# A fused attention and MLP kernel: products written in place and gathered from there, and a plan over two batches and the first channel MLP

## The chip, the cores and the metric

The kernel runs on one core of a Trainium2 chip. The metric is the device time of one execution in microseconds (us), the median of the runs shown; lower is better. The core has TensorE (PE; PEld is its weight load), VectorE (DVE), ScalarE (ACT), GpSimd (POOL) and SyncE (SP), which here issues nearly all DMA transfers.

## The reference

Batch 4, 8 heads, sequence 768, head dimension 48, model width 384. Three parts follow each other.

- Attention as a recurrence with a complex decay per channel: the decay's magnitude is clipped at 0.999, the state takes `k v` at each step, and `q` reads the state's real part.
- A mixer: `u = x + (U V)` applied along the sequence (rank 32, the "token mix"), then a channel MLP, `u + relu(u w_ch1) w_ch2` with 1536 hidden columns.
- A second mixer: `theta = x w_theta`, `x cos(theta)` and `x sin(theta)` go through two 768x768 matrices along the sequence, and a channel layer with relu is added.

```python
new_re = ar * S_re - ai * S_im
new_im = ar * S_im + ai * S_re
S_re, S_im = (new_re + kv, new_im)
y[:, :, t] = np.einsum('bhd,bhde->bhe', q[:, :, t], S_re)
...
h = xt @ U @ V
u = x + h.transpose(0, 2, 1)
ch = np.maximum(u @ w_ch1, 0.0) @ w_ch2
```

## The kernel before

The recurrence is worked in chunks of 128 positions, six to a batch, with attention matmuls inside a chunk and a carried 48x48 state per head between chunks. The decay's powers come from a scan of the magnitude and a scan of the angle.

**Preparing a pair of chunks** (`ew`, L276, on 128x768 tiles). `load` (L254) brings four rows `re`, `im`, `q`, `kk`, in three transfers for each of the two chunks, the last with q and k together. ACT squares, takes reciprocal roots, arctangent and sine; DVE multiplies and scans (L315 for the magnitude, L346, three times, for the angle). Four more rows A, B, C, D are used for the squares first and for the sine and cosine at the end. POOL clears a column of `dec` (L298), copies the scan's last column (L324, choice of POOL or ACT) and writes a sentinel column into the product buffer (L370). For each chunk, `prod` (L374) multiplies q and k by the sine and by the cosine, into a buffer `SRC` of its own: there is one such buffer, and a second for the odd chunks of batch 0. `gather` (L380) moves each half to the tile `QK` by five transfers on SP (L387 to L391), so ten for a chunk.

**A chunk on PE** (`pe_steps`, L405): scores (L431), which ACT copies (L437) and POOL masks (`affine_select`, L441); transposes of k (L447, copied by ACT at L399); the state (L470); the output (L496, and L499 for the carried state), copied into `x` by ACT (L399); and the first half of the token mix (L511). After six chunks, `g_steps` (L524) closes the token mix: one evacuation by ACT (L530) and one by DVE (L533), six matmuls (L541) and six additions on DVE (L546).

**Weights.** `unpack` (L553) turns 64-bit weights into a high and a low fp32r part: one load, five integer steps (L573 to L580; the first may go to ACT, at L574), a cast on ACT (L587), and the low part, `lo = value - hi`, which may go to POOL or DVE (L588, recorded at L272). Nine such jobs make `w1`, twelve make `w2`, one `U` and one `V`. Their staging is memory of `x` of batch 1. The second mixer's weights are unpacked the same way after the attention of batch 3 (lane `w3`).

**The channel MLP** of a batch (`mains`, L759) has 18 units: `f_unit` (18 matmuls of 128x256 at L659; ACT makes the high part with relu at L664, DVE the low part at L665) and `c_unit` (12 matmuls of 128x384 at L680), one unit behind. Before every six units `prologue` transposes x (L641) and splits it (L645, L646).

**What sets the order.** `startup` (L719) collects the steps of batch 0's attention (`PLANNED = 1`), the token mix and the weights. `schedule` (L80) gives each step an engine and a place: it takes ready steps in the order of a rank (the table `LEAD`) and puts each into the first free gap on its engine's line, even ahead of steps placed before. `fixed` (L689) emits them in that order and ties each DVE, ACT and POOL instruction to the one before it on its engine (`HELD`, L688); PE and SP aren't tied. Everything else is emitted in lanes of falling priority, `evac a0 a1 a2 a3 w3 moe p2 mix fill`, and the framework's list scheduler may put it between the planned steps: attention of batch 1 in lane `a1`, the MLPs in `moe`, and so on, where the attention of a batch stands above the MLP of the batch ahead of it.

## Time and profile before

| What | Value |
|---|---|
| median of 3 runs | 890.32 us (889.41 to 893.34) |
| the profiled execution | 890.87 us, of which the span is 889.0 us |
| PE busy | 772.3 us, 87% of the span |
| DVE busy | 534.5 us, 60% |
| ACT busy | 437.2 us, 49% |
| POOL busy | 214.7 us, 24% |
| DMA | 79.69 MB, mean 90 GB/s |

The busy shares are means over stages that differ. The span has three: the start-up, in which batch 0's attention and the weights are made ready; the stretch in which the MLPs and the attention of batches 1 to 3 share PE; and the second mixer from 655 us on. The granted clock is a share of TensorE's full 2.4 GHz; 0.5 stands for 1.2 GHz, values between are means.

### The profile page before, as it was taken

Reading aid. Unit: us, or ns where it says so; the run is one execution under the profiler, and the core shown is the slowest. Engines: PE = TensorE matmul, PEld = TensorE weight load, DVE = VectorE, ACT = ScalarE, POOL = GpSimd, SP = SyncE. Lnnn points to the kernel's source line nnn. Section 1 sums busy time; section 2 is a strip of 40 time slices with the busy share of each in tenths; the row PEclk is TensorE's granted clock in tenths of the full one; section 3 lists DMA queues with packets and bytes.
Section 4 is the critical chain, followed back from the end, with each engine's and each line's share of the span. In section 5 each row is a group of like instructions: output and inputs, shape, how many; then the busy total and the mean of one; then the engine's idle time right before and its main releaser. Section 6 shows DMA issues by size and latency. Waiting matters only on the chain.

```text
span 889.0 us, 13548 instructions
## 1 busy us (share of the span) xinstructions
PE 772.3 (87%) x5242; PEld 745.9 (84%) x5242; DVE 534.5 (60%) x763; ACT 437.2 (49%) x703; POOL 214.7 (24%) x218
## 2 busy tenths in 40 slices
PE   0167565689999989999999899999999999999996
PEld 0166454689889889898998899999999999999996
DVE  7989979994857748867177785332234434354321
ACT  5766836484946956965233442221145435343300
POOL 2032443232202112313012232000044424224200
PEclk9996765899999999999999999999999999999999
DMA  9345646434443434452216741000050000000001
GB/s 250 104 120 156 191 128 171 114 84 116 107 116 81 126 100 113 110 125 52 83 54 209 237 159 37 1 1 1 1 204 11 28 27 1 27 27 28 28 28 31
DMA packets 104889, 79.69 MB, mean 90 GB/s; under 512 B 32144, under 2 KB 96656, under 8 KB 104816
## 3 DMA queue, kind: packets, MB, share of 16 engines
q1 hardware_dynamic: 104416, 78.55, 31.7%
q8 instruction: 43, 0.70, 0.3%
q14 instruction: 30, 0.25, 0.1%
q10 hardware_dynamic: 400, 0.20, 0.1%
HBM read 50.33 MB, written 9.44 MB: 67 GB/s over the span
## 4 chain that ended last, share of the span: by engine, by line
PE 51%; DVE 17%; ACT 14%; DMA 7%; issue 4%; SPq 4%; POOL 2%; DVEq 0%; POOLq 0%; ACTq 0%
PE c L680 9%; PE h L659 9%; PE h L906 8%; PE c L906 8%; ACT et L293 4%; PE m L855 4%; PE m L922 4%; PE m L496 2%; SPq L387 2%; ACT L293 2%; DVE SRC L272 2%; PE m L499 2%; DVE et L296 2%; DMA tok1l<-tl 1%; DMA ei<-in_pk_dram 1%
## 5 line engine op out<-in xcount | busy, mean ns | idle before, releaser
L659 PE MATMUL h<-uh,w1h 128*128 128x256 f32 x432 | 123.7, 286 | 5.1 <-DVE ul L646 4.1
L659 PE MATMUL h<-uh,w1l 128*128 128x256 f32 x432 | 122.8, 284 | 0.0
L659 PE MATMUL h<-ul,w1h 128*128 128x256 f32 x432 | 122.6, 284 | 0.2 <-DVE ul L646 0.2
L665 DVE SCALAR_TENSOR_TENSOR rl<-h,rh 128x512 fp32r<-128x512 f32 x72 | 49.6, 688 | 102.7 <-ACT rh L664 102.4
L680 PE MATMUL c<-w2h,rl 128*128 128x384 f32 x288 | 99.9, 347 | 0.8 <-DVE rl L665 0.7
L680 PE MATMUL c<-w2l,rh 128*128 128x384 f32 x288 | 99.1, 344 | 0.0
L680 PE MATMUL c<-w2h,rh 128*128 128x384 f32 x288 | 95.7, 345 | 0.8 <-ACT rh L664 0.8
L431 PE MATMUL m<-QK 96*128 96x128 f32 x384 | 56.8, 298 | 44.3 <-DMA QK<-SRC 40.5
L664 ACT ACTIVATE rh<-h 128x512 fp32r<-128x512 f32 x72 | 42.9, 598 | 104.0 <-PE h L659 103.9
L431 PEld LDWEIGHTS m<-QK 96*128 96x128 f32 x384 | 52.1, 210 | 48.8 <-issue 44.2
L659 PEld LDWEIGHTS h<-uh,w1h 128*128 128x128 f32 x432 | 81.4, 188 | 6.7 <-DVE ul L646 5.0
L659 PEld LDWEIGHTS h<-ul,w1h 128*128 128x128 f32 x432 | 81.4, 188 | 0.7 <-DVE ul L646 0.4
L659 PEld LDWEIGHTS h<-uh,w1l 128*128 128x128 f32 x432 | 81.4, 188 | 0.3
L496 PE MATMUL m<-vt,pt 128*128 128x96 f32 x384 | 64.9, 298 | 2.5 <-POOL pt L441 2.4
L441 POOL TENSOR_SCALAR_AFFINE_SELECT pt<-pt 128x512 f32<-128x512 f32 x48 | 46.6, 978 | 75.9 <-ACT pt L437 75.5
L470 PE MATMUL m<-vt,kn 128*96 128x96 f32 x320 | 38.7, 272 | 25.5 <-ACT kn L399 24.6
L272 DVE TENSOR_TENSOR SRC<-ei,et 128x768 f32<-128x768 f32 x40 | 41.3, 1071 | 31.7 <-POOL SRC L370 30.7
L470 PEld LDWEIGHTS m<-vt,kn 128*96 128x96 f32 x320 | 34.3, 182 | 30.9 <-ACT kn L399 28.7
L496 PEld LDWEIGHTS m<-vt,pt 128*128 128x128 f32 x384 | 56.8, 213 | 3.8 <-POOL pt L441 3.8
L680 PEld LDWEIGHTS c<-w2h,rl 128*128 128x128 f32 x288 | 54.7, 190 | 2.2 <-DVE rl L665 2.0
L680 PEld LDWEIGHTS c<-w2l,rh 128*128 128x128 f32 x288 | 54.7, 190 | 0.3
L680 PEld LDWEIGHTS c<-w2h,rh 128*128 128x128 f32 x288 | 53.1, 189 | 1.4 <-ACT rh L664 1.0
(210 smaller groups left out, 1910.9 us busy)
## 6 DMA issues: line engine op xcount, KB each, us to landing
QK<-SRC SPq DMA_DIRECT2D x84, 144.6 KB, 3.4
ei<-in_pk_dram SPq DMA_DIRECT2D x44, 192.0 KB, 2.9
ei<-in_pk_dram SPq DMA_DIRECT2D x22, 384.0 KB, 3.8
x<-in_moe_w_ch_dram SPq DMA_DIRECT2D x9, 512.0 KB, 4.5
vt<-in_v_dram SPq DMA_DIRECT2D x24, 192.0 KB, 3.1
x<-in_moe_w_ch_dram SPq DMA_DIRECT2D x12, 384.0 KB, 3.8
st<-in_moe_w_tok_i_dram SPq DMA_DIRECT2D x6, 768.0 KB, 5.3
st<-in_moe_w_tok_r_dram SPq DMA_DIRECT2D x6, 768.0 KB, 4.2
```

Of the source, the lines that this page charges most:

```text
L272: ENG[e].tensor_tensor(**kw)
L293: do("A", size, r, w, lambda e: A_.activation(out=out, in_=in_, func=func, **kw), tab)
L431: PE.matmul(ps[:, hh * T:(hh + 1) * T], lhsT=st["QK"][:, h, T:2 * T], rhs=st["QK"][:, h, 0:T], start=True, stop=True)
L441: G_.affine_select(out=pt, in_=pt, pattern=[[0, 4], [1, T]], compare_op=ALU.is_ge, fill=0.0, base=0, channel_multiplier=-1)
L470: PE.matmul(ps[0:96, r * 96:(r + 1) * 96], lhsT=st["kn"][:, h, :], rhs=vw(h), start=(z == 0), stop=(z == 1))
L496: PE.matmul(o, lhsT=st[f"pt{h // 4}"][:, h % 4, :], rhs=vw(h), start=(z == 0), stop=(z == 1 and c == 0))
L659: PE.matmul(ps[:, f, :], lhsT=a[:, k, fs], rhs=u[:, k, :], start=(k == 0 and i == 0), stop=(k == NJ - 1 and i == 2))
L664: A_.activation(out=rh, in_=ps, func=AF.Relu)
L665: V_.scalar_tensor_tensor(out=rl, in0=ps, scalar=0.0, in1=r32(rh), op0=ALU.max, op1=ALU.subtract)
L680: PE.matmul(ps[t][:, 0:C], lhsT=r[:, f, t * T:(t + 1) * T], rhs=w[:, k, :], start=(k == 0 and i == 0), stop=(k == KF - 1 and i == 2))
L855: PE.matmul(ps[:, 0:C], lhsT=a[:, k, :], rhs=ww[:, k, :], start=(k == 0 and i == 0), stop=(k == NJ - 1 and i == 2))
L906: PE.matmul(ps[k][:, 0:C], lhsT=z[:, 2 * part + o, k * 128:(k + 1) * 128], rhs=w[:, s, ts], start=(s == 0 and part == 0 and j == 0), stop= ...
```

## The change

- **Rows and products.** The pair's store becomes twelve padded rows of 6x129 elements; q and k, and C and D, lie beside each other, so that the products of a chunk are written in place: with the sine into C and D, with the cosine into q and k. `gather` reads from there; `SRC` is gone. There is a second row for `im`, used by pairs in turn, and rows `n` and `sq` that the angle and the square use. The column that POOL cleared is cleared once at the start. The sentinel and the copy of the scan's last column are always on ACT. q and k, and the halves of the value tile, are loaded by transfers of their own.
- **Unpacking.** The first step is always on ACT, the low part always on DVE. Staging moves to the memory of batch 2's `x`.
- **The plan.** `PLANNED = 2`, and the first batch's MLP (`mlp_steps`) is part of it, each piece a step with its own keys (`w1` by column group, `w2` by row block, the PSUM banks `ph` and `pc`). `schedule` goes forward in time: among the ready steps that could start within 400 ns of the earliest, it takes the one of lowest rank, and nothing is put ahead of a step already placed. Ranks are a step's distance from the end along its dependencies plus `LEAD`, which has new values. `HELD` stays the same.

```diff
-PLANNED = 1
+PLANNED = 2
...
-def schedule(steps, rank, bias, hop=HOP, banks=4, pf=1.3, warm=1e5):
+COST = {"V": (150, 1.042), "A": (180, 0.833), "G": (150, 2.1), "P": (0, 1.0), "D": (0, 1)}
+BANKS = {"ps": 4, "ph": 2, "pc": 2}
+def schedule(steps, rank, bias, hop=HOP, window=400):
...
+            cand.append((best, n))
+            low = min(low, best[1])
+        (_, st, en, e), n = min((c for c in cand if c[0][1] <= low + window), key=lambda c: (rank[c[1]], c[1]))
...
+def ranks(steps, names, lead, hop=HOP):
...
+        up[n] += a + b * size + hop[e]
+        for m in pre[n]:
+            up[m] = max(up[m], up[n])
...
+        out.append((top - up[n]) / 1000 + r0 + dr * k / names.count(nm))
...
-    stg = [xf[:, NC * C + i * 1536:NC * C + (i + 1) * 1536] for i in range(3)]
-    src2 = xf[:, B * NC * C - NJ * 2 * (2 * T + 1):]
+    stg = [xf[:, PLANNED * NC * C + i * 1536:PLANNED * NC * C + (i + 1) * 1536] for i in range(3)]
...
+    ROWS = ("re", "im", "q", "kk", "A", "B", "C", "D", "dec", "n", "sq", "im1")
+    er = ac.tile([128, len(ROWS), NR], F32, name="er")
...
-    EU = 'AV'
+    EU = 'A'
...
-        for lo, hi, names in ((0, 1, ("re",)), (1, 2, ("im",)), (2, 4, ("q", "kk"))):
+        zi = (1, 11)[pr % 2]
+        for z, name in enumerate(("re", ROWS[zi], "q", "kk")):
...
+            for z in range(2):
+                nc.sync.dma_start(out=vt[:, :, 2 * z, :], in_=v[b, z::2, c * T:(c + 1) * T, :].rearrange("r s e -> s r e"))
...
-        do("G", 3, [], K("dec"), lambda e: G_.memset(dec[:, :, :, 0:1], 0.0))
...
-        do("GA", 6, K("dec"), [("pc", pr)], pcs)
+        do("A", 6, K("A"), [("pc", pr)], lambda e: A_.copy(out=pcf[:, pr], in_=rows[4][:, :, T]))
...
+        for a, key in (("qk", "kk"), ("cd", "D")):
+            do("A", 6, K("C"), K(key), lambda e, a=a: A_.mul(
+                out=st[a][:, :, 1, T], in_=st["cd"][:, :, 0, T - 1], mul=P2_0 ** -0.5))
...
-            do("GA", 6, K("C"), [sk + "0", sk + "1"], src)
...
+            for cs, to, a, keys in ((1, "cd", n2, ("C", "D")), (0, "qk", Bt, ("q", "kk"))):
+                kc = K(*[(x, i) for x in keys])
+                tt2(st[to][:, i::2, :, 0:T], st["qk"][:, i::2, :, 0:T],
+                    a[:, i::2].rearrange("p j (o t) -> p j o t", o=1).to_broadcast([128, NJ, 2, T]), ALU.mult,
+                    K("q", "kk", ("q", i), ("kk", i), "nB"[cs == 0]), K(*(keys if i == 0 else ())) + kc)
+                do("D", 3250, kc + K(*keys), [f"qk{g % 2}{cs}"], lambda e, g=g, cs=cs: gather(e, g, cs))
...
-        do("GV", n, lambda e: tt(e, out=lo, in0=tv, in1=r32(hi), op=ALU.subtract), w)
+        do("V", n, lambda e: tt(e, out=lo, in0=tv, in1=r32(hi), op=ALU.subtract), w)
...
+    def mlp_steps(b):
...
+            do("P", 18 * 119, [("u", n % 2)] + [("w1", p // 2, k) for k in range(NJ)], [m], mm)
+            do("A", 512, [m], [kr], hi)
+            do("V", 512, [m, kr], [kr, m], lo)
...
+                do("P", 6 * 174, [kr, ("w2", 2 * p), ("w2", 2 * p + 1)], [m], lambda e, t=t: mm(e, t))
...
+        ops = mlp_steps(0)
+        steps.extend(ops)
+        names.extend("m0" if o[1] == "P" else "mv" for o in ops)
+        rank = ranks(steps, names, LEAD)
         done = schedule(steps, rank, BIAS)
...
-        mains(b)
+        if b:
+            mains(b)
```

## Rows read from the trace of the kernel before

**Rows 1.** The page, part 4: the chain that ended last, by engine.
```profile
PE 51%; DVE 17%; ACT 14%; DMA 7%; issue 4%; SPq 4%; POOL 2%; DVEq 0%; POOLq 0%; ACTq 0%
```

**Rows 2.** Stretches: length; PE, PEld, DVE, ACT, POOL busy; granted clock; DMA; GB/s.
```profile
0.00:169.00 169.00, 81.72 (x472) 72.73 (x472) 147.73 (x206) 108.53 (x155) 54.83 (x63) 0.78 0.59 156
40.50:90.00 49.50, 37.08 (x223) 34.20 (x224) 44.90 (x57) 31.94 (x50) 15.61 (x16) 0.82 0.51 138
90.00:138.00 48.00, 28.70 (x182) 25.90 (x180) 40.39 (x61) 26.85 (x40) 21.94 (x15) 0.68 0.60 163
138.00:169.00 31.00, 15.95 (x70) 12.60 (x70) 29.31 (x47) 22.57 (x33) 10.27 (x10) 0.57 0.47 134
169.00:655.00 486.00, 464.21 (x3450) 448.11 (x3451) 296.04 (x399) 241.72 (x372) 87.74 (x86) 1.00 0.33 90
655.00:889.00 234.00, 226.33 (x1322) 225.02 (x1320) 90.69 (x159) 86.99 (x178) 72.10 (x70) 0.99 0.13 41
```

**Rows 3.** Timeline of PE, 0 to 230 us; in brackets wait and releaser.
```profile
118.21 1.59 PE L470 MATMUL m<-vt,kn 128*96 128x96 f32 x8 [14.52 <-ACT kn L399]
...
169.42 0.39 PE L659 MATMUL h<-uh,w1h 128*128 128x256 f32 x1 [3.06 <-DVE ul L646]
```

**Rows 4.** The chain of waits between 85 and 175 us: start, length, what.
```profile
88.03 1.82 DVE x L272 x2
...
160.91 1.40 DVE x L546 x3
```

**Rows 5.** Timeline of SP's queue, 80 to 200 us: start, length, issue.
```profile
100.62 0.65 SPq L387 DMA_DIRECT2D QK<-x  x1
```

**Rows 6.** Timeline of POOL, 85 to 200 us.
```profile
103.15 10.35 POOL L324 COPY pcf<-dec 128x6 f32<-128x6 f32 x1 [4.83 <-DVE dec L315]
```

**Rows 7.** The page, its part 6: DMA issues, KB each, us to landing.
```profile
QK<-SRC SPq DMA_DIRECT2D x84, 144.6 KB, 3.4
ei<-in_pk_dram SPq DMA_DIRECT2D x44, 192.0 KB, 2.9
ei<-in_pk_dram SPq DMA_DIRECT2D x22, 384.0 KB, 3.8
```

**Rows 8.** Groups of DVE, 0 to 190 us: count, busy us, mean ns, idle.
```profile
L578 DVE SCALAR_TENSOR_TENSOR x<-x 128x384 uint32<-128x384 uint32 x12 | 10.1, 840 | 0.2
...
L272 DVE TENSOR_TENSOR ei<-ei,et 128x768 f32<-128x768 f32 x8 | 7.3, 952 | 0.0
L315 DVE TENSOR_TENSOR_SCAN dec<-dec,d 128x774 f32<-128x774 f32 x4 | 7.1, 1764 | 0.1
L272 DVE TENSOR_TENSOR ei<-ei,et 128x1536 f32<-128x1536 f32 x4 | 7.0, 1752 | 0.0
...
L573 DVE TENSOR_SCALAR x<-x 128x384 uint32<-128x384 uint32 x10 | 3.9, 394 | 0.0
...
L346 DVE TENSOR_TENSOR_SCAN et<-ones,ei 128x256 f32<-128x256 f32 x6 | 3.7, 669 | 0.3 <-ACT ei L343 0.3
...
L546 DVE TENSOR_TENSOR x<-x,m 128x384 f32<-128x384 f32 x6 | 3.0, 547 | 0.0
...
L272 DVE TENSOR_TENSOR w1l<-x,w1h 128x512 fp32r<-128x512 f32 x3 | 2.0, 675 | 1.8 <-ACT w1h L587 1.8
```

**Rows 9.** DVE's busy time on staging and x, 169 to 190 us.
```profile
169.00:190.00 21.00, 11.66 (x19) 1.00 0.42 114
```

**Rows 10.** Groups of POOL over the span, columns as in 8.
```profile
L272 POOL TENSOR_TENSOR w2l<-x,w2h 128x384 fp32r<-128x384 f32 x12 | 14.6, 1216 | 31.7 <-ACT w2h L587 31.6
...
L272 POOL TENSOR_TENSOR w1l<-x,w1h 128x512 fp32r<-128x512 f32 x6 | 9.3, 1544 | 13.8 <-ACT w1h L587 13.8
```

**Rows 11.** The chain of waits between 545 and 565 us, in the MLPs alone.
```profile
557.10 2.11 PE c L680 x12
559.21 2.13 PE h L659 x18
```

**Rows 12.** Who waited for whom over the span: us, times, longest.
```profile
DVE SRC L272 <- POOL SRC L370: 30.7, 13, 6.3
```

More of the change, by code (lines that the diff above doesn't have):

```diff
@@ L89, in schedule @@
             succ[m].append(n)
-    uses = {}
+    uses, psn = {}, []
     for _, _, _, r, w, _ in steps:
-        for k in {*r, *w}:
-            if k[0] == "ps":
-                uses[k] = uses.get(k, 0) + 1
-    psn = [sorted(k for k in {*s[3], *s[4]} if k[0] == "ps") for s in steps]
-    bank, free = {}, [0.0] * banks
-    line = {e: ([], [], []) for e in "VAGPD"}
-    end = [0.0] * len(steps)
-    heap = [(rank[n], n) for n in range(len(steps)) if not left[n]]
-    heapq.heapify(heap)
-    out, wait = [], []
@@ L149, in schedule @@
         out.append((st, n, e, en))
+        ready.remove(n)
         for k in psn[n]:
@@ L517, in pe_steps @@
         gk = [gps["k"]] if b else []
[L519 to L520 removed]
+        mix.append(step(lambda e: copy(e, xs[b][:, c, :], st["y"][:, 0:C]), "A", 384, [m], [m, ("x", b, c)]))
         mix.append(step(gx, "P", 660, [("x", b, c), "u4"], [kg] + gk))
@@ L759, in mains @@
     def mains(b):
-        units = [(n, p) for n in range(NB) for p in range(KF // 2)]
-        prologue(b, 0)
-        for i, (n, p) in enumerate(units):
-            f_unit(b, n, p)
-            if i:
-                c_unit(b, *units[i - 1])
-            if p == 3 and n + 1 < NB:
-                prologue(b, n + 1)
-        c_unit(b, *units[-1])
+        for f, e, *_ in mlp_steps(b):
+            with lane("moe" if e == "P" else "evac"):
+                f(e)
     with lane("a0"):
```

428 lines of the change are left out of this document (219 added, 209 removed), and 23 rows, old and new, of the table LEAD.

## The prediction

> **What bounds the kernel now.** I read the chain that ended last first, to see which engine holds the end. It is TensorE for 51% of the span, VectorE (DVE) for 17%, ScalarE (ACT) for 14% [rows 1]. The stretches then show where each rules [rows 2]. From 169 us to 655 us PE is busy 464.2 of 486 us, and from 655 us to the end 226.3 of 234: 690.5 us of work and 29.5 us of idle time, at a granted clock of 0.99 to 1.00. There only less PE work or less idle time helps, and the change takes no PE work out. Before 169 us it is otherwise: PE is busy 81.7 us at a clock of 0.78, while DVE is busy 147.7 of 169 us. So the first 169 us belong to DVE and to the order of the work, and the question is when the first channel MLP, the start of the full stretch, can begin.
>
> The timelines of single engines say why it begins only at 169.4 us [rows 3]. The last products of batch 0 are done at 89.85 us [rows 4], 79.6 us earlier. What should follow is one gather, one chunk of attention and the token mix. Instead, the gather of the last chunk is issued at 100.62 us [rows 5]; a 128x6 copy of batch 1 holds the POOL queue for 10.35 us [rows 6], with a mask of batch 0 and the sentinel fill behind it; a matmul of batch 0 then waits 14.52 us, because the copy that feeds it stands in ACT's fixed order behind a weight cast, which waits for DVE, which waits for that fill [rows 3]; and the last three additions of the token mix come at 160.91 us [rows 4], behind steps of batch 1. Batch 1 is not in the plan of before: its instructions are put between the planned ones, on queues whose order the plan has fixed.
>
> **The change part by part.**
>
> *Batch 1 and the first MLP in the plan.* By the trace's durations the tail after 89.85 us needs: ten gather issues at about 0.63 us, 6.3 [rows 5]; landing 3.4 [rows 7]; about 5 us of PE (a whole chunk is at most 15.95 x 0.57 = 9.1 us at full clock, the PE time of 138 to 169 us [rows 2]); and eight evacuations of about 0.6 us [rows 8], 4.8; with hand-overs some 12 us after the landing. That is 111.5 us; I take 115 for the MLP's start, as some of this will not run freely. Ends: 105 if batch 0's products also come earlier, 145 if the weights go ahead of them.
>
> *What DVE must do first.* The MLP's first six units need all first- and second-layer weights. DVE has spent 147.7 us by 169, of which batch 1 took some 32. A pair of chunks costs 13 steps of 0.952, one of 1.752, a scan of 1.764 and three of 0.669: 17.9 us [rows 8]; pair 3 whole and pair 4 without its four products (3.8) make 32. Another 11.7 us of weight steps lie behind 169 [rows 9]. So 147.7 - 32 + 11.7 = 127 us. The change adds the low-half subtractions that POOL had: 6 x 0.675 + 12 x 0.547 = 10.6 us. It takes away the first unpack step, 14 times about 0.394: 5.5 us [rows 8]; ACT gets those, busy 108.5 of 169 us [rows 2], and has room. And what POOL's subtractions cost DVE goes: the 12 shifts of 384 columns took 0.840 us where another two-input step of that size took 0.547 [rows 8], 3.5 us in this one group. Ends for all groups: 0, and the 23.9 us that POOL spent there [rows 10]; I take 7, twice the one group, since other groups beside it show less. 127 + 10.6 - 5.5 - 7 = 125 us. At the share that DVE reached while the plan ran alone, 44.9 of 49.5 [rows 2], with 5 us for the MLP's own evacuations, that is 130 / 0.907 = 143 us; for what the two batches get out of order I add 5: 148.
>
> The shift row also bears on a rule. The Trainium skill ("SBUF — State Buffer", section "Who interferes with whom") says that a DVE instruction with two SBUF inputs contends with a GpSimd instruction that reads SBUF, and that the later one is blocked for the whole instruction. By it most of POOL's 23.9 us would be DVE's loss, the weights would be ready some 17 / 0.907 = 19 us sooner, and the sum would lose the 7.6 us of idle time below: 850 us; 0.840 against 0.547 agrees with the rule in direction, not in that size.
>
> *PE between 115 and 148.* It can do six units at 2.13 + 2.11 us [rows 11], 25.4 of 33 us: 7.6 idle. At a clock of 0.82, which 75% busy had [rows 2], they still fit.
>
> *Rows of their own, products in place.* The single product buffer goes; DVE waited 30.7 us for its fill in 13 places [rows 12], most of them after 169 us, where the MLP covers them (PE 95.5% busy): nothing there. Next pair's squares no longer write over this pair's angles. New waits: the loads of the next q and k stand behind this pair's gathers on SP. That is 3.2 us of issue, 3.4 to land, 2.9 to load [rows 7], about 10, while DVE needs eight steps and a scan, 9.4 us [rows 8], to reach the product that reads them: 0, with 2 us in each of five planned pairs as the other end, 10. Behind those loads SP holds value loads and weight loads, which are an iteration early. ACT gets three small copies a pair that POOL had; the POOL queue keeps only the masks, so no mask stands behind a scan any more.
>
> *More and smaller transfers.* q and k split 384 KB into two of 192 KB, and each value load becomes two: 24 more in the plan's 6 pairs. SP pays at most 0.65 us an issue [rows 5], 16 us spread over some 250, hidden by its idle time; 2 x 2.9 in place of 3.8 us [rows 7], 2 us a pair, is the other end, 12 us if each pair waits. The Trainium skill ("DMA: Bandwidth & Descriptors", section "Rules for kernel authors") tells to coalesce transfers, which speaks against this edit; were its fixed cost of about 2 us paid by each pair, the sum would be 12 us higher, the same as that end.
>
> *After 148 us.* PE has 12 units (51 us) and six chunks (8 us each: 100 together), DVE three pairs (54) and some 39 additions and low halves of 0.55 us or more (22): 76 against 100, PE bound again. For an order that is now fixed on three engines I add the idle share of the whole middle, 4.5%, once more: 5 us. The low halves of the last weights move from POOL to DVE too, under the MLPs of 455 to 600 us: nothing.
>
> **Sum.** From the MLP's start: 690.5 us, one chunk more that was already done at 169 (8), idle 29.5 + 7.6 + 5 = 42: 741. 115 + 741 = 856 us of span, against 889.0; with the 1.87 us that lie around the span in the profiled run (890.87), 858. The median of the three runs is 0.55 lower than that run, which I leave aside.
>
> **The rivals.**
> 1. *The weights go first.* The start moves to 145 us only, as DVE's bill must be paid anyway; the 7.6 us fall away: 145 + 733 = 878, 880 us. For it: DVE is the fuller engine before 169. Against: the first unit needs three of nine first-layer pieces.
> 2. *Slower: the fixed order starves PE.* In the planned stretch after 115 us lie 18 units and six chunks, 76 + 49 = 125 us of PE work, on three queues that cannot overtake. The forecast gives them about 145 us, 86% (with 7 us of the middle's idle time). At the 60% of 90 to 138 us (28.7 of 48) they need 209: 64 more, 922 us. At the 75% of 40.5 to 90, 167: 22 more, 880. Slower by 0.5% begins at about 69%. For it: the 14.52 us wait was such a queue [rows 3]. Against: that wait came from steps outside the plan.
> 3. *Better.* Start at 105 us, no idle time for weights, half of the middle's idle time saved: 105 + 698.5 + 29.5 - 10 = 823 of span at best, 825; with half of these gains, about 838.
> 4. *It does not do what it says.* PE's order is not among the held ones; if its matmuls of the MLP are queued behind waiting ones of batch 1, the start stays near 165 us: 890.
>
> **How the numbers follow.** Forecast 0.58, with 838 to 872 from the two 10 to 12 us ends and 105 to 125 us of start; rival 1 0.18 (872 to 886); rival 3 0.09; rival 2 0.10; rival 4 0.05. A measurement of this kernel tells about 0.5% from no change (its three runs differ by 0.4%). Faster takes the forecast, rivals 1 and 3 nearly whole, 0.84; same 0.06; slower 0.10. The range leaves out part of rivals 2 to 4: 834 to 886.
>
> **What would show it.** The first MLP matmul between 105 and 125 us; no POOL subtraction of weights, shifts near 0.56 us; DVE's weight steps done by about 150 us; PE busy over 85% from 115 to 260 us at a clock of 1.0; the work after the first MLP's end unchanged in length. A start after 140 us, or a share below 70% there, would make the prediction wrong.

## The result, and the profile after

The changed kernel takes 877.24 us (median of 4 runs, 876.67 to 877.70) where the kernel before takes 890.81 (889.41 to 893.34, 4 runs): a ratio of 0.9844, 95% interval 0.982 to 0.9868. That is 13.6 us faster. The forecast was 858 us and 33 us of gain; the direction holds, the size does not.

The chain that ended last, by engine, as in [rows 1]: TensorE (PE) holds more of it than before.

```profile
PE 59%; DVE 17%; DMA 8%; ACT 7%; SPq 4%; issue 4%; POOL 1%; DVEq 0%; ACTq 0%
```

Stretches of the changed kernel, columns as in [rows 2]:

```profile
0.00:131.00 131.00, 63.05 (x416) 57.19 (x416) 108.96 (x152) 95.33 (x149) 17.97 (x36) 0.86 0.60 160
131.00:181.00 50.00, 48.41 (x364) 46.88 (x364) 40.78 (x78) 24.44 (x46) 3.24 (x4) 0.96 0.45 127
181.00:238.00 57.00, 56.20 (x402) 54.92 (x403) 46.16 (x59) 39.74 (x64) 2.13 (x2) 1.00 0.27 72
238.00:290.00 52.00, 39.65 (x227) 34.88 (x226) 33.72 (x45) 27.05 (x45) 6.89 (x7) 0.73 0.41 100
290.00:400.00 110.00, 105.23 (x818) 99.91 (x818) 85.46 (x113) 74.59 (x127) 16.69 (x13) 0.99 0.44 112
400.00:500.00 100.00, 98.84 (x766) 95.53 (x765) 47.86 (x77) 37.68 (x64) 7.57 (x10) 1.00 0.33 90
500.00:640.00 140.00, 135.64 (x929) 134.22 (x928) 72.67 (x109) 46.75 (x75) 2.57 (x3) 0.98 0.25 87
640.00:875.00 235.00, 227.87 (x1332) 226.48 (x1330) 90.62 (x159) 86.54 (x177) 71.84 (x70) 1.00 0.13 41
```

From 131 to 238 us PE is full (104.6 of 107 us). Then comes what the kernel before does not have, a hole: from 238 to 290 us PE is busy 39.65 of 52 us, at a granted clock of 0.73, and DVE idles too, 33.72 busy of 52. From 290 us on PE is nearly full again (105.23 of 110).

The PE timeline, as in [rows 3]: the first MLP matmul starts at 131.40 us in place of 169.42.

```profile
106.55 2.13 PE L451 MATMUL m<-QK 96*128 96x128 f32 x16
...
114.31 1.17 PE L516 MATMUL m<-vt,pt 128*128 128x96 f32 x4 [5.62 <-POOL pt L461]
...
131.40 0.58 PE L696 MATMUL h<-uh,w1h 128*128 128x256 f32 x1 [1.68 <-DVE ul L677]
```

To see where the head start goes I count work. The number of matmuls of each kind in a stretch, times what one takes at full clock (0.119 and 0.1755 us for the two products of the MLP, 2.13/18 and 2.11/12 [rows 11]; 0.086 to 0.325 us for attention's kinds), gives the full-clock work that PE has done by a given time, out of 503 us in all before the second mixer:

| by (us) | 131 | 181 | 238 | 290 | 400 | 500 | 640 |
|---|---|---|---|---|---|---|---|
| before | 41.3 | 64.6 | 117.9 | 164.5 | 264.8 | 360.6 | 485.1 |
| after | 47.2 | 92.9 | 148.7 | 175.3 | 277.4 | 375.3 | 500.1 |
| ahead | 5.9 | 28.3 | 30.8 | 10.8 | 12.6 | 14.7 | 15.0 |

The head start reaches 30.8 us of work, close to the forecast gain, and 20 us of it are given back between 238 and 290 us. The rest stays to the end. So there are two questions: what made the head start, and why it was lost in that hole.

Who does what around the hole stands in DVE's timeline: the last low half of the weights and the magnitude scan of pair 4 behind it, the last addition of the first MLP, the first token-mix addition of batch 1.

```profile
181.37 0.55 DVE L309 TENSOR_TENSOR w2l<-x,w2h 128x384 fp32r<-128x384 f32 x1
181.84 1.76 DVE L356 TENSOR_TENSOR_SCAN er<-er,d 128x774 f32<-128x774 f32 x1
...
238.29 0.54 DVE L726 TENSOR_TENSOR x<-x,c 128x384 f32<-128x384 f32 x1
...
282.60 1.02 DVE L566 TENSOR_TENSOR x<-x,m 128x384 f32<-128x384 f32 x2
```

The first MLP is done at 238 us, 112 us earlier than before (350). The second may only start behind batch 1's token mix, which begins at 283 us, 21 us later than before (261.4). In the plan pair 4 of batch 1 stands behind the weights: its scan, now at 181.84 us, came at 152.08 in the kernel before:

```profile
152.08 1.76 DVE L315 TENSOR_TENSOR_SCAN dec<-dec,d 128x774 f32<-128x774 f32 x1
...
397.36 1.75 DVE L315 TENSOR_TENSOR_SCAN dec<-dec,d 128x774 f32<-128x774 f32 x1
```

The second of these lines is the scan of the last pair of batch 3. After the change it comes at 391.18 us:

```profile
391.18 1.76 DVE L356 TENSOR_TENSOR_SCAN er<-er,d 128x774 f32<-128x774 f32 x1
```

The MLP began 38 us earlier, but the last scan of attention came only 6 us earlier, and the token mixes of batches 1, 2 and 3 began 21, 29 and 18 us later (table below).

### The profile page after: what moved, and what is told of

Same layout as the page of the kernel before. It is cut to its first block, busy times and chain, and to the rows that moved or that the text cites. A ratio compares the mean times of both kernels' runs of the same rounds, so it can differ in the third digit from the quotient of the medians.

```text
span 875.0 us, 13559 instructions
## 1 busy us (share of the span) xinstructions
PE 774.9 (89%) x5242; PEld 750.0 (86%) x5242; DVE 526.2 (60%) x786; ACT 432.1 (49%) x741; POOL 128.9 (15%) x144
## 4 chain that ended last, share of the span: by engine, by line
PE 59%; DVE 17%; DMA 8%; ACT 7%; SPq 4%; issue 4%; POOL 1%; DVEq 0%; ACTq 0%
PE h L696 10%; PE c L721 9%; PE h L956 9%; PE c L956 9%; DVE er L335 6%; PE m L905 4%; PE m L972 4%; PE m L516 3%; ACT er L332 3%; PE m L519 3%; DMA QK<-er 2%; PE m L451 2%; DMA tok1l<-tl 2%; PE m L490 2%; SPq L295 1%
## 5 line engine op out<-in xcount | busy, mean ns | idle before, releaser
L696 PE MATMUL h<-uh,w1h 128*128 128x256 f32 x432 | 125.7, 291 | 4.2 <-DVE ul L677 4.2
L696 PE MATMUL h<-ul,w1h 128*128 128x256 f32 x432 | 125.1, 290 | 0.1
L461 POOL TENSOR_SCALAR_AFFINE_SELECT pt<-pt 128x512 f32<-128x512 f32 x48 | 51.9, 1091 | 395.3 <-ACT pt L457 395.1
L335 DVE TENSOR_TENSOR er<-er 128x768 f32<-128x768 f32 (+1 forms) x99 | 104.2, 1078 | 4.1 <-DMA er<-in_pk_dram 2.0
L696 PEld LDWEIGHTS h<-uh,w1h 128*128 128x128 f32 x432 | 83.9, 194 | 5.7 <-DVE ul L677 5.1
L332 ACT ACTIVATE er<-er 128x768 f32<-128x768 f32 x88 | 73.9, 845 | 28.4 <-DVE er L335 17.8
L696 PEld LDWEIGHTS h<-uh,w1l 128*128 128x128 f32 x432 | 83.7, 194 | 0.3 <-issue 0.2
L516 PE MATMUL m<-vt,pt 128*128 128x96 f32 x384 | 62.6, 290 | 11.9 <-POOL pt L461 11.7
L338 DVE SCALAR_TENSOR_TENSOR er<-er 128x768 f32<-128x768 f32 x55 | 52.5, 961 | 22.1 <-ACT er L332 6.9
L467 PE MATMUL m<-ident,QK 96*128 96x96 f32 x160 | 23.5, 272 | 41.4 <-DMA QK<-er 40.8
L467 PEld LDWEIGHTS m<-ident,QK 96*128 96x128 f32 x160 | 19.4, 158 | 45.1 <-issue 42.8
```

Of the source, the lines that this page charges most:

```text
L332: do("A", size, r, w, lambda e: A_.activation(out=out, in_=in_, func=func, **kw), tab)
L335: do("V", size, r, w, lambda e: V_.tensor_tensor(out=out, in0=in0, in1=in1, op=op))
L338: do("V", size, r, w, lambda e: V_.scalar_tensor_tensor(out=out, in0=in0, scalar=scalar, in1=in1, op0=op0, op1=op1))
L461: G_.affine_select(out=pt, in_=pt, pattern=[[0, 4], [1, T]], compare_op=ALU.is_ge, fill=0.0, base=0, channel_multiplier=-1)
L467: PE.transpose(ps[:, hh * 96:(hh + 1) * 96], st["QK"][:, 4 * i + hh, 1, 0:T], ident[0:96, 0:96])
L516: PE.matmul(o, lhsT=st[f"pt{h // 4}"][:, h % 4, :], rhs=vw(h), start=(z == 0), stop=(z == 1 and c == 0))
```

## The experiments

Eighteen kernels ran, each beside the kernel before on the same chip (medians of that one: 889.7 to 890.8). "MLP" is the first MLP's first matmul and its last addition; "mix" the first token-mix addition of batches 1, 2 and 3, each from the profiled run.

| run | median us | ratio, 95% interval | MLP | mix 1, 2, 3 |
|---|---|---|---|---|
| before | 890.8 | | 169 to 350 | 261, 351, 446 |
| after | 877.2 | 0.982 to 0.987 | 131 to 238 | 283, 381, 464 |
| e1, MLP not planned | 927.2 | 1.037 to 1.046 | 203 to 398 | 283, 391, 470 |
| e16, one batch planned | 903.1 | 1.012 to 1.018 | 169 to 304 | 308, 398, 483 |
| e6, MLP outside the order | 876.5 | 0.977 to 0.988 | 131 to 255 | 275, 383, 465 |
| e2, batch 2 held | 876.5 | 0.979 to 0.989 | 134 to 234 | 263, 413, 495 |
| e9, second MLP needs no mix | 868.6 | 0.973 to 0.977 | 133 to 241 | 290, 399, 481 |
| e3, cosine rows, new order | 905.6 | 1.013 to 1.022 | 136 to 255 | 295, 396, 492 |
| e5, cosine rows, stale column | 881.4 | 0.984 to 0.994 | 131 to 237 | 280, 376, 463 |
| e14, cosine rows | 880.1 | 0.986 to 0.992 | 133 to 239 | 281, 378, 465 |
| e4, low halves on POOL | 888.8 | 0.997 to 1.001 | 134 to 243 | 286, 381, 467 |
| e7, no clamp | 885.8 | 0.993 to 0.997 | 129 to 234 | 279, 390, 472 |
| e8, first step on DVE | 894.3 | 1.004 to 1.007 | 134 to 244 | 285, 398, 480 |
| e15, masks on DVE | 881.7 | 0.986 to 0.992 | 133 to 240 | 285, 382, 471 |
| e10, values on POOL | 884.2 | 0.988 to 0.994 | 136 to 243 | 286, 391, 475 |
| e11, all loads on POOL | 899.4 | 1.006 to 1.012 | 136 to 246 | 292, 403, 487 |
| e12, SP in plan order | 885.4 | 0.993 to 0.996 | 133 to 241 | 287, 382, 467 |
| e13, tail ahead | 890.3 | 0.998 to 1.002 | 138 to 244 | 286, 391, 474 |
| e17, imaginary row behind | 880.0 | 0.987 to 0.991 | 134 to 237 | 279, 383, 468 |
| e18, values behind too | 882.6 | 0.989 to 0.993 | 134 to 237 | 282, 387, 472 |

### What makes the head start: e16, e1, e6

e16 plans one batch (the staging of the weights goes back to batch 1's `x` with it, as in the kernel before):

```diff
-PLANNED = 2
+PLANNED = 1
```

> The changed kernel with batch 0 and the first MLP alone in the plan; batch 1's steps are unplanned again, as in the kernel before. Theory A (planning batch 1 behind the MLP and the weights is what makes it late): batch 1's token mix ends before 282 us, by 10 us or more, with a start of the MLP between 131 and 150 us, and the time is 865 to 880. Rival (without a plan batch 1's steps get in between batch 0's, as in the kernel before): the start is later than 145 us and the time is 880 to 895.

The rival holds, and by more than it said: 903.1 us. The PE timeline of this kernel has a stall like that of the kernel before [rows 3], and the start falls back to 168.5 us:

```profile
147.75 1.17 PE L516 MATMUL m<-vt,pt 128*128 128x96 f32 x4 [21.40 <-POOL pt L461]
...
168.50 0.58 PE L696 MATMUL h<-uh,w1h 128*128 128x256 f32 x1 [0.24 <-DVE ul L677]
```

The mask that PE waits for follows ACT's copy of the scores, which comes only at 146.25 us, behind a weight cast, with DVE on steps of batch 1 and of the weights until then. With the MLP planned and batch 1 not, there is no head start at all. Batch 1's steps between batch 0's are what held the MLP back, as the prediction read it. The run also shows that an early pair 4 does not by itself give an early mix: its scan comes at 126.4 us here, 55 us earlier than in the changed kernel, and batch 1's mix 25 us later.

e1 takes the MLP out of the plan:

```diff
-        ops = mlp_steps(0)
-        steps.extend(ops)
-        names.extend("m0" if o[1] == "P" else "mv" for o in ops)
...
-        if b:
-            mains(b)
+        mains(b)
```

> The changed kernel with the first channel MLP taken out of the plan: both batches stay planned, and the MLP's steps are given to the same lanes as the other three MLPs, behind the plan in priority. Theory A (the 31 us of head start that the MLP had at 225 us is given back because its steps and its weights stand ahead of batch 1's attention on DVE): batch 1's token mix ends earlier than 282 us, by 10 us or more, the first MLP ends later than 238 us, TensorE has no hole between 238 and 290 us, and the time is at most 877 us, as low as 862. Rival B (the planned MLP is the whole gain, rows and planner bring nothing): the first MLP matmul falls back to 150 us or later and the time goes to 886 to 893. A time between, with a start near 131 us, would say that the plan for two batches does it alone.

Both were wrong: the start is 203 us and the time 927.2. The ranks are counted back from the end of the plan, and without the MLP behind it nothing makes batch 0's token mix urgent: its additions come at 196 to 210 us, where the changed kernel has them at 127 to 145. So this run says nothing of theory A; by this reading it is the MLP's place at the end of the chain that orders everything before it. e6 separates that from the fixed order of the MLP's own steps:

```diff
-        return fixed([(steps[n][0], e, (st, n)) for st, n, e, _ in done])
+        return fixed([(steps[n][0], e, (st, n)) for st, n, e, _ in done if names[n] not in ("m0", "mv")])
...
-        if b:
-            mains(b)
+        mains(b)
```

> The same plan, computed with the first MLP in it, but the MLP's own steps are left out of the fixed order and given to the lanes of the other three MLPs. Batch 0 and batch 1 keep the order that the plan gave them. Theory A (what helps is the order that the plan makes before the MLP, what hurts is that the MLP's DVE and ACT steps stand in a fixed order with batch 1's): the MLP still starts at 130 to 136 us, batch 1's token mix ends 8 us or more before 282 us, and the time is 862 to 872. Rival E (the fixed order of the MLP's steps is itself the gain): the start or the first units slip by 10 us or more and the time is 882 to 895.

The start stays (131.0 us), batch 1's mix comes 7 us earlier, the MLP ends 17 us later, and the time, 876.5 (870.2 to 880.1), is the same. To the time it does not matter, within the spread of the runs, whether the MLP's steps stand in the fixed order; next to e1 it matters that the plan was made with them in it.

### What the hole costs, and who fills it: e9 and e2

e9 lets the second MLP work on batch 0's activations; batch 1 then has no channel MLP:

```diff
+        bx = 0 if b == 1 else b
...
-                                     xs[b][:, 2 * n + t, (k0 + kk) * 128:(k0 + kk + 1) * 128], ident)
+                                     xs[bx][:, 2 * n + t, (k0 + kk) * 128:(k0 + kk + 1) * 128], ident)
...
-                x = xs[b][:, 2 * n + t, :]
+                x = xs[bx][:, 2 * n + t, :]
```

> The changed kernel with the second channel MLP reading and adding to batch 0's activations in place of batch 1's: it does the same work but need not wait for batch 1's token mix (batch 1 then has no channel MLP, and batch 0 has two). Theory A (the head start is lost because TensorE has nothing to do between the end of the first MLP at 238 us and the end of batch 1's attention at 288 us): TensorE is busy over 95% at full clock from 238 to 290 us, and the time falls by 12 to 20 us, to 857 to 865. Rival G (the pace of the attention of batches 2 and 3 sets the end, and work taken up earlier is missed later): the hole moves to the stretch in which batch 2's attention is still under way and the time stays within 4 us of 877.

868.6 us: 8.6 less than the changed kernel, between what the two theories said. Its stretches:

```profile
238.00:290.00 52.00, 47.51 (x367) 45.39 (x366) 39.01 (x52) 33.01 (x55) 5.82 (x6) 0.97 0.41 100
290.00:400.00 110.00, 98.41 (x716) 94.39 (x715) 70.83 (x95) 70.67 (x113) 34.56 (x12) 0.91 0.43 109
```

The hole is filled (47.5 us at 0.97 in place of 39.65 at 0.73), so the missing token mix is its cause. By the count above PE has done 193.4 us of work at 290 us, 18.1 more than the changed kernel. But at 400 us it has done 283.1 against 277.4, only 5.7 more: with the MLPs further ahead, PE now runs short while batch 2's attention is under way. Its longest waits there, about half of what it loses, and POOL's timeline:

```profile
PE m L516 <- POOL pt L461: 10.3, 5, 4.9
```

```profile
340.17 10.66 POOL L461 TENSOR_SCALAR_AFFINE_SELECT pt<-pt 128x512 f32<-128x512 f32 x2 [11.19 <-ACT pt L457]
355.85 0.63 POOL L461 TENSOR_SCALAR_AFFINE_SELECT pt<-pt 128x512 f32<-128x512 f32 x1 [5.02 <-ACT pt L457]
...
368.58 12.58 POOL L461 TENSOR_SCALAR_AFFINE_SELECT pt<-pt 128x512 f32<-128x512 f32 x2 [9.05 <-ACT pt L457]
```

e2 attacks the hole from the other side: the first step of batch 2 on DVE, ACT and POOL goes behind the last planned one.

```diff
+                if i.engine in hold:
+                    tc.add_manual_dep(i, hold.pop(i.engine).name, mybir.DependencyInfo(
+                        mybir.DependencyClass.NoSync, mybir.DependencyReason.DATA), reason="plan")
...
```

> The changed kernel with batch 2's first steps on DVE, ACT and POOL put behind the last planned step of the same engine. Theory C (the unplanned steps of batch 2 get in between the planned ones and delay batch 1, as batch 1 did in the kernel before): batch 1's token mix ends 5 to 15 us earlier than 282 us and the time falls by 3 to 10 us, to 867 to 874. Rival A (batch 1 is late for its own chain of waits, and DVE idles anyway): batch 1's token mix moves by less than 3 us, batch 2 starts later, and the time is the same or up to 8 us longer, 876 to 885.

Each theory got one half. Batch 1's six additions come 19.6 us earlier, more than theory C said, and the time is the same, as rival A said:

```profile
263.05 2.87 DVE L566 TENSOR_TENSOR x<-x,m 128x384 f32<-128x384 f32 x6 [0.53 <-PE m L561]
```

```profile
238.00:290.00 52.00, 43.82 (x321) 39.30 (x320) 24.29 (x35) 30.94 (x48) 3.81 (x6) 0.97 0.31 77
290.00:400.00 110.00, 96.46 (x706) 91.14 (x707) 81.98 (x103) 76.72 (x124) 22.59 (x12) 0.93 0.42 107
```

At 290 us PE is 13.4 us of work ahead of the changed kernel (188.7), at 400 us 0.9 behind it (276.5): batch 2's first scan comes 37 us later (272.5 for 235.3) and its mix 32 us later.

Both runs point the same way. Attention is a stream of pairs that feeds the MLPs. By its last scan its pace hardly changed with the MLP's start (6 us); most of the work that PE takes up earlier is missing later, while it waits for the next batch. e2 also shows what makes batch 1's mix late: 20 us of it are steps of batch 2 that run ahead of it. Clearing them out only moves the lateness to batch 2.

### The in-place rows: e3, e5, e14

The chain of waits of the changed kernel goes through the edit that I had put at 0: gathers of pair 4 land, only then the loads of pair 5's q and k are issued, and DVE takes them up.

```profile
223.71 3.21 DMA QK<-er
...
228.07 3.57 DMA er<-in_pk_dram
...
233.63 1.75 DVE er L335
```

e3 moved the cosine products to rows that are dead by then:

```diff
-            for cs, to, a, keys in ((1, "cd", n2, ("C", "D")), (0, "qk", Bt, ("q", "kk"))):
+            for cs, to, a, keys in ((1, st["cd"], n2, ("C", "D")), (0, cq, Bt, ckey)):
...
```

> The changed kernel with the cosine products of q and k written over the rows of the imaginary parts and of the scanned magnitudes, which are dead by then, in place of over q and k themselves (two zeroings of 6 columns a pair go to POOL, and the copy of the last column to its new place comes after the angle scans). The loads of the next q and k then wait for the products alone, no longer for the gathers. Theory D (the in-place rows are on the chain of batch 1, and cost some 10 us of wait a pair where I had put 0): the waits of DVE for the q and k rows around 231 and 275 us go, batch 1's token mix ends 8 us or more earlier, and the time falls by 4 to 12 us, to 865 to 873. Rival (that wait only takes the place of another one): the time stays within 3 us of 877.

905.6 us, 28 longer. The edit gives the plan other steps and keys, and with the same ranks it comes out as another order: batch 0's mix ends 13 us later, the first MLP 17 us. The wait itself was not tested. e5 and e14 keep every planned step in its place and take batch 3's activations as the free rows for pairs 4 to 8:

```diff
+        cq = ep if 4 <= pr < 9 else st["qk"]
...
-            for cs, to, a, keys in ((1, "cd", n2, ("C", "D")), (0, "qk", Bt, ("q", "kk"))):
+            for cs, to, a, keys in ((1, st["cd"], n2, ("C", "D")), (0, cq, Bt, ("q", "kk"))):
...
```

> The cosine rows once more, now with every planned step of the changed kernel at its old place in the order: for pairs 4 to 8 the cosine products go to a free stretch of batch 3's activations (the staging area of the weights, which is done with by then), so the loads of the next q and k wait for the products alone. Theory D (the wait for the gathers was on the chain, and the run before was only slower for another order of the plan): DVE's waits on the loads of q and k around 231 and 275 us go, batch 1's token mix ends 5 to 15 us before 282 us, and the time is 865 to 873. Rival (the wait only takes the place of another): within 3 us of 877.

In this run the last column of q and k that goes with the cosine rows was a stale one, copied before its source was made; the next has it in its place:

> The cosine rows with the old order again, with the copy of the last column back at its old step, behind the product that it copies from (in the run before it stood ahead of it, so that this column was a stale one). Theory D: as before, batch 1's token mix 5 to 15 us before 282 us and 865 to 873. Rival (the run before, 881 with batch 1's mix at 280 us, told the truth: the wait for the gathers only takes the place of another one): 874 to 884.

881.4 and 880.1 us, a little above the changed kernel. What DVE waited for from 181 to 290 us, in the changed kernel:

```profile
DVE a_st L501 <- PE m L490: 13.0, 1, 13.0
...
DVE er L338 <- DMA er<-in_pk_dram: 3.2, 1, 3.2
DVE er L335 <- DMA er<-in_pk_dram: 2.0, 1, 2.0
DVE er L338 <- ACT er L332: 1.9, 1, 1.9
```

and in e14 (its L341, L335 and L508 are L338, L332 and L501 of the changed kernel):

```profile
DVE a_st L508 <- PE m L497: 14.0, 1, 14.0
DVE er L341 <- ACT er L335: 5.1, 2, 3.2
```

The 5.2 us of waits for loads are gone, the wait of the same steps for ACT has grown from 1.9 to 5.1 us, and batch 1's mix moves by 1.4 us. On the chain by the trace, worth nothing in time: the rival holds, and for pairs 4 to 8, which alone were moved, the 0 of the prediction too.

### DVE's bill: e4, e7, e8

```diff
-        do("V", n, lambda e: tt(e, out=lo, in0=tv, in1=r32(hi), op=ALU.subtract), w)
+        do("V", n, lambda e: tt("G", out=lo, in0=tv, in1=r32(hi), op=ALU.subtract), w)
```

> The changed kernel with the low-half subtractions of the weights issued on POOL again, at the same place of the plan. By the terms of my sum DVE loses 10.6 us of work before the weights are done and pays some 7 us for POOL beside it: the weights are done 0 to 6 us earlier than 181 us and the time is 873 to 879. Rival (POOL blocks DVE for most of the 24 us that POOL spent there): the shifts of 384 columns go back to about 0.84 us, DVE's weight steps end 8 us or more later than 181 us, and the time is 882 to 895.

888.8 us, 11.6 longer: the rival's time, but not by its way. Groups of DVE over the span, first of the changed kernel, then of e4 (columns as in [rows 8]):

```profile
L598 DVE SCALAR_TENSOR_TENSOR tl<-st,tl 128x768 uint32<-128x768 uint32 (+1 forms) x16 | 14.4, 901 | 0.1
...
L598 DVE SCALAR_TENSOR_TENSOR x<-x 128x384 uint32<-128x384 uint32 (+2 forms) x22 | 14.0, 638 | 0.7
L595 DVE TENSOR_SCALAR x<-x 128x384 f32<-128x384 f32 (+2 forms) x22 | 9.0, 407 | 1.1 <-ACT x L594 1.1
...
L596 DVE TENSOR_SCALAR x<-x 128x384 uint32<-128x384 uint32 (+2 forms) x22 | 8.7, 396 | 0.6
```

```profile
L598 DVE SCALAR_TENSOR_TENSOR tl<-st,tl 128x768 uint32<-128x768 uint32 (+1 forms) x16 | 25.3, 1579 | 0.4
L598 DVE SCALAR_TENSOR_TENSOR x<-x 128x384 uint32<-128x384 uint32 (+2 forms) x22 | 15.2, 692 | 0.7
...
L596 DVE TENSOR_SCALAR x<-x 128x384 uint32<-128x384 uint32 (+2 forms) x22 | 12.0, 544 | 0.7
L595 DVE TENSOR_SCALAR x<-x 128x384 f32<-128x384 f32 (+2 forms) x22 | 11.0, 499 | 4.0 <-ACT x L594 4.0
```

Beside POOL's subtractions the planned unpacking (tile x) costs DVE 1.2 + 3.3 + 2.0 = 6.5 us more, where I had taken 7. The shifts of the late weights (tile tl) cost 10.9 more, which I had not looked at; from 470 us on PE waits 7.1 us for the MLP's low parts from DVE, where it waited 0.4 in the changed kernel. e7 leaves the clamp out, e8 puts the first step back on DVE, both for the planned weights alone:

```diff
-        do("V", n / 2, lambda e: V_.tensor_scalar(out=tf, in0=tf, scalar1=PAT_HI, scalar2=PAT_LO, op0=ALU.min, op1=ALU.max), wt)
+        do("V", n / 2, lambda e: None if keys else V_.tensor_scalar(out=tf, in0=tf, scalar1=PAT_HI, scalar2=PAT_LO, op0=ALU.min, op1=ALU.max), wt)
```

```diff
-        do(EU, n / 2, lambda e: V_.tensor_scalar(out=t, in0=w_hi, scalar1=0x7FFFFFFF, scalar2=None, op0=ALU.bitwise_and) if e == "V" else
+        do(EU, n / 2, lambda e: V_.tensor_scalar(out=t, in0=w_hi, scalar1=0x7FFFFFFF, scalar2=None, op0=ALU.bitwise_and) if e == "V" or keys else
```

> The changed kernel without the clamp step (minimum and maximum) in the planned unpacking of the weights: some 21 DVE steps of about 0.39 us, 8 us of DVE work before 181 us, the order untouched. The clamp is left out of the computation. Theory F (until batch 1 is done the time belongs to DVE's bill): DVE's weight steps end 8 us or more before 181 us and the time falls by 6 to 12 us, to 865 to 871. Rival (batch 1's chain of gathers, loads and hand-overs is as long as before): the weights are earlier, the time falls by 3 us at most.

> The changed kernel with the first unpacking step of the planned weights back on DVE, at the same place in the order: by my sum 14 to 21 steps of 0.39 us, 5.5 to 8 us more on DVE, and as much less on ACT. Theory F: DVE's weight steps end 5 to 9 us later than 181 us and the time is 882 to 887. Rival: within 3 us of 877.

In the planned stretch both do what the bill says: the last low half comes at 176.2 and 186.7 us in place of 181.4, the first MLP ends 4.7 us earlier and 5.5 us later. Behind it the sign is lost. e8 is 17 us longer, three times its cost; e7, with 8 us less work, is 8.6 us longer, for batch 2's mix comes 9.6 us later. In e7 a pair of masks took 10 us at 334 us, and PE waited 9.7 us for POOL between 290 and 400, where the changed kernel has no such wait among its longest:

```profile
334.45 10.00 POOL L461 TENSOR_SCALAR_AFFINE_SELECT pt<-pt 128x512 f32<-128x512 f32 x2 [13.31 <-ACT pt L457]
```

So theory F is right up to 240 us and says nothing of the end. As I read it, the steps of batches 2 and 3 are put around the plan when the program is built, and a change ahead of them gives them other neighbours.

### Masks, queues, the tail: e15, e10, e11, e12, e17, e18, e13

e15 makes the masks of batches 2 and 3 on DVE:

```diff
+            if b >= PLANNED:
+                V_.tensor_tensor(out=pt, in0=st[f"s{i}"].rearrange("p (h t) -> p h t", h=4),
+                                 in1=tri.rearrange("p (o t) -> p o t", o=1).to_broadcast([128, 4, T]), op=ALU.mult)
+                return
...
```

> The changed kernel with the masks of batches 2 and 3 made by one DVE product from PSUM with a constant triangle, in place of ACT's copy and POOL's select. A select takes 0.64 us when DVE is idle and up to 6 us where DVE's two-input steps stand beside it. 24 masks of about 0.7 us are 17 us more on DVE and 14 us less on ACT, after 285 us. Theory P (attention's pace after 285 us is set in part by POOL's selects): batch 3's token mix ends 4 us or more before 464 us and the time falls by 3 to 10 us. Rival (DVE is the fuller engine there and pays): the time is the same or up to 8 us longer.

881.7, and batch 3's mix 6 us later: the rival. (The 6 us of the expectation were two selects in one row; the longest single one of the changed kernel took 4.76 us.) e10 and e11 issue loads from POOL's queue, e12 fixes SP's order as well:

```diff
-                nc.sync.dma_start(out=vt[:, :, 2 * z, :], in_=v[b, z::2, c * T:(c + 1) * T, :].rearrange("r s e -> s r e"))
+                nc.gpsimd.dma_start(out=vt[:, :, 2 * z, :], in_=v[b, z::2, c * T:(c + 1) * T, :].rearrange("r s e -> s r e"))
```

```diff
-                    nc.sync.dma_start(out=to, in_=pk[b, 2 * c + i, :, z])
+                    nc.gpsimd.dma_start(out=to, in_=pk[b, 2 * c + i, :, z])
```

```diff
-    HELD = ('DVE', 'Activation', 'Pool')
+    HELD = ('DVE', 'Activation', 'Pool', 'SP')
```

> The changed kernel with the value loads issued from POOL's queue in place of SP's. In the changed kernel SP stood 45 us in 13 waits of a value load for matmuls that still read the buffer, with gathers and loads of q and k behind it (7.56 us at 260 us). Theory H (SP's one queue delays the gathers, which are on the chain of batch 1): batch 1's token mix ends 3 us or more before 282 us and the time falls by 3 to 8 us, to 869 to 874. Rival (the gathers wait for DVE's products anyway): within 3 us of 877.

> The changed kernel with the value loads and the loads of the four rows of each pair issued from POOL's queue; SP keeps the gathers and the weights. At 237 to 246 us a load of the next imaginary row waited 8.1 us on SP for DVE's scan with the finished products' gathers behind it. Theory H: batch 1's token mix ends 8 us or more before 282 us, and the time is 865 to 872. Rival (POOL's queue holds the masks, and a load that waits there keeps them back, or the loads issued there land later): PE's waits for POOL's masks grow by 8 us or more and the time is 878 to 890.

> The changed kernel with SP's planned transfers held in the plan's order too, as DVE, ACT and POOL are. Theory H: SP's waits get shorter, batch 1's token mix ends earlier than 282 us by 3 to 10 us and the time is 868 to 874. Rival (the plan takes 2 us from issue to landing where the trace shows 2.9 to 3.4, so its order of transfers is no better than the one found without it): within 3 us of 877, or slower.

884.2, 899.4 and 885.4: none brought batch 1's mix forward. e12 fits its rival; e10 and e11 are slower than either of their sides said, and why is open: in e11 PE waits for masks only 3.7 us from 131 to 640 us. e17 and e18 leave the loads on SP and hold them back behind the gathers (e18 also the values behind their own pair's q and k):

```diff
...
+                    if z == 1 and pr >= PLANNED * NQ:
+                        behind(last_q[pr], last_g[pr - 2])
...
```

> The changed kernel with one edit to SP's order from batch 2 on: the load of a pair's imaginary row, which can be issued two pairs ahead since there is a second such row, may not stand ahead of the gathers of the pair two before it. In the changed kernel the load of pair 8 stood 8.1 us on SP for pair 6's scan (237 to 245 us), with the finished products of pair 5 behind it. Theory H (that queue, not DVE's bill, holds up the last gathers of batch 1): the first gather of pair 5 is issued at 240 to 242 us in place of 246.8, batch 1's token mix ends 4 to 7 us before 282 us, and the time falls by 3 to 8 us, to 869 to 874. Rival A (attention is late by its whole chain, and one wait less lets the next come out): batch 1's mix moves by less than 3 us and the time stays within 3 us of 877.

> The same, and from batch 2 on the value loads stand behind the loads of their own pair's q and k on SP; in the changed kernel two pairs of them stood 7.56 us at 260 us for matmuls that still read the buffer, with pair 6's q and k behind them. Theory H: DVE's wait for q and k at 274 us goes as well, batch 2's token mix ends 4 us or more before 380 us, and the time is 866 to 872. Rival A: within 3 us of 877; or the values now come late, PE waits for them for 5 us or more, and the time is 878 to 886.

880.0 and 882.6. In e17 the load no longer stands in front, and the first gather of pair 5 is still issued at 246.0 us (246.8 in the changed kernel): it waited for DVE's product. Batch 1's mix does come 4.0 us earlier, but not by that way, and the time does not follow: theory H falls. e13 moved the tail of batch 0 up in the order:

```diff
+            key[n], eng[n] = st - (8000 if names[n] in ('p5', 'x4', 'x5', 'u', 'g0') else 0), e
...
```

> The changed kernel, its plan's order kept except that the steps of batch 0's last chunk, of its token mix and of the first token-mix factor move up by 8 us of planned time where their inputs allow it. In the changed kernel ACT takes up the two masks of that chunk 4 to 5 us after their scores are done, behind weight casts, table loads and steps of batch 1, and the MLP starts at 131 us where I had put 115. Theory S (the late start is the missing term, and what is won there stays): the first MLP matmul comes 4 to 8 us earlier, at 123 to 127 us, and the time falls by as much, to 869 to 873. Rival A (the start is worth nothing while batch 1's attention ends at 282 us, for TensorE only runs dry earlier): the start moves, batch 1's token mix does not, and the time stays within 3 us of 877.

It missed its aim: the mix began no earlier (128.8 us), and the MLP's own first low half fell behind other steps.

```profile
137.87 0.58 PE L696 MATMUL h<-uh,w1h 128*128 128x256 f32 x1 [6.23 <-DVE ul L677]
```

So the worth of an earlier start was not measured. No version beat both kernels: e2 and e6 are within the spread of the changed kernel, and e9 computes something else.

## Why the prediction was wrong

**The start, 115 us: 131.4 measured.** Batch 0's tail went forward for the reason given (e16), but 16 us less far. The sum had the last gather landed at 99.6 us and 12 us from there to the MLP; it landed at 106.2, and the rest took 25, to 131.4. The scores of the last chunk end at 108.7 us, and ACT copies them at 112.95 and 114.08, behind weight and pair 3 steps in its fixed order:

```profile
107.17 1.28 ACT L332 ACT_TABLE_LOAD   x1
...
109.22 0.49 ACT L607 CAST w2h<-x 128x384 fp32r<-128x384 f32 x1
...
112.95 0.57 ACT L457 COPY pt<-m 128x512 f32<-128x512 f32 x1
...
114.08 0.57 ACT L457 COPY pt<-m 128x512 f32<-128x512 f32 x1
```

PE has waited 5.62 us by then, and from 114.31 to 120 us its granted clock is 0.50, the lower level; the last chunk and the first token-mix factor are done at 125.7 us, 11.4 us where the sum had 5 for PE. That the later landing, this order and this clock make up the 16 us is read from the rows, not shown by a run.

**DVE's bill and the weights by 148: 181.4.** The work terms were about right. The shifts of 384 columns take 0.558 us (forecast 0.56), POOL's part is 6.5 us (forecast 7), the first step on ACT 5.5 us (e8, by the end of the first MLP). What I did not see is that the plan puts pair 3 of batch 1 (17.9 us [rows 8]) ahead of the last weights, and that DVE would be busy 149.7 of 181 us, a share of 0.83 where the sum had 0.907: (130 + 17.9) / 0.83 is some 178 us. Up to 238 us it cost nothing: in place of the 7.6 us of idle time between 115 and 148, PE is idle 2.4 of 107 us from 131 to 238. That makes up for much of the late start, and the head start is 30.8 us, close to the forecast because two misses cancel, which is luck. Behind 238 us the late weights do count: pair 4's scan follows the last low half (181.37 and 181.84 us), and in e7 and e8, where that low half came 5 us earlier and 5 us later, batch 1's mix came 3.4 us earlier and 2.8 us later.

**In-place rows 0, split transfers 0.** The first is confirmed by e14 for pairs 4 to 8, with the wait plainly on the chain of the trace. The second was not tried alone; a load of 192 KB now takes 3.6 us to land (2.9 before, and 3.8 for 384 KB [rows 7]).

**The step that failed: "After 148 us".** "76 against 100, PE bound again", with 5 us of idle time. In its place stands the hole between 238 and 290 us: PE does 26.6 us of full-clock work in 52 us and so loses 25, of which 12.35 us are idle time and the rest goes with the granted clock of 0.73; 20 us of the head start are given back. I compared busy times, DVE's 76 us with PE's 100, as if the work could be taken up in any order. The size was right, DVE is busy 80 of the 109 us from 181 to 290. But the second MLP needs the whole of batch 1, whose last two pairs are a chain of gathers, scans and hand-overs that takes 101 us from the scan of pair 4 (181.8) to the token mix (282.6). It took 109 us before (152.1 to 261.4): hardly shorter now, it starts 30 us later, while the first MLP ends 112 us earlier. e9 shows that this dependency makes the hole, and e2 that steps of batch 2 make up 20 us of the chain. Of the rivals, the first gives the nearest time (880) by the wrong way, as the start did not wait for the weights; the second, an order that starves PE, is nearest in kind, and its line at 75% gives 880 us as well, but from 131 to 238 us PE was 98% busy, and it starved only when the planned MLP was over. One slip in the working: half of rival 3's gains is about 842 us, not 838; nothing here hangs on it.

**What stays open.** How batch 1's mix could come earlier without batch 2 coming later. The in-place rows (e14), the order of the MLP's steps (e6), loads in front of gathers (e17) and DVE's clamp (e7) were taken away one at a time, and its mix moved by 1 to 8 us; only holding batch 2 back moved it by 20 (e2), and then batch 2 was late. The clock may have a part: from 247.3 to 265.3 us, in batch 1's last chunks, PE is busy 16.94 of 18 us at a granted clock of 0.53, and DVE's longest wait, 13.0 us, is for those matmuls; no run isolates this. What sets the end is not shown either. In 15 of the 18 runs the time is batch 3's first mix addition plus 409 to 422 us, but that does not make the pace of attention the cause: e2 and e9 break the rule (382 and 388 us), and in e2 that mix comes 31 us later at the same time. The new scheduler and its ranks stand in all eighteen runs, so their own share is not known.

## What to carry to other kernels

A head start is worth what the next dependency leaves of it. Before counting it to the end, ask what the following stage needs, when that is ready, and whether its chain, not its busy time, got shorter. And where part of a program is ordered anew at each build, an experiment that removes 8 us of work can come out 9 us slower: read such a run by the stretch that it changes, and believe its total only to about 10 us. That holds for e9's 8.6 us too, and for differences of 3 to 8 us among the runs above; what they show stands in the columns of the table and in the stretches.

## What was not expected of the hardware

POOL's mask takes 0.63 us alone, and two of them took 10.66 and 12.58 us together in e9, the longest single one 7.41 us. DVE's timeline beside the second pair shows steps with two inputs nearly back to back, with a few short others between them:

```profile
368.44 1.76 DVE L356 TENSOR_TENSOR_SCAN er<-er,d 128x774 f32<-128x774 f32 x1
370.12 2.67 DVE L335 TENSOR_TENSOR er<-er 128x768 f32<-128x768 f32 x3
...
378.84 1.82 DVE L338 SCALAR_TENSOR_TENSOR er<-er 128x768 f32<-128x768 f32 x2
```

The masks end at 381.2, when DVE's row of such steps ends. The Trainium skill ("SBUF — State Buffer", section "Who interferes with whom") says that a DVE instruction with two SBUF inputs contends with a GpSimd instruction that reads SBUF, that the port pair they share is an exclusive lock, and that the order of issue decides who blocks. The trace agrees in kind, and its size is more than one DVE step: the longest here is 1.76 us, so by the rows these masks were kept out through several in a row. The other direction is in e4: with the low-half subtractions on POOL, a 768-column shift takes 1.73 us on average in place of 0.95. First e4, then the changed kernel, shapes kept apart:

```profile
L598 DVE SCALAR_TENSOR_TENSOR tl<-st,tl 128x768 uint32<-128x768 uint32 x14 | 24.2, 1726 | 0.4
L598 DVE SCALAR_TENSOR_TENSOR tl<-st,tl 128x768 uint32<-128x768 uint32 x14 | 13.3, 952 | 0.1
```

I had used this rule only for what POOL costs DVE; what it costs the masks, and through them PE, was the larger surprise.
